# A retention layer ahead of a leaky feed-forward: state sums, visit and next scores of a pair in one run of 64x64 products

## The chip, the cores and the metric

The kernel runs on one core of one Trainium2 chip. The metric is the device time of one launch in microseconds. A core has a matrix engine (TensorE, PE in the profile, with PEld for its weight loads), two engines for elementwise work (VectorE, DVE; ScalarE, ACT), a general engine (GpSimd, POOL) and a queue that issues transfers (SyncE, SP). TensorE writes to eight PSUM banks, from which VectorE and ScalarE read.

## The reference

```python
# q, k, v: (4, 8, 768, 64); w_in: (512, 2048); w_out: (2048, 512)
gamma = 1.0 - 2.0 ** (-5.0 - np.arange(H))
for t in range(S):
    state = gamma[None, :, None, None] * state + np.einsum('bhd,bhe->bhde', k[:, :, t], v[:, :, t])
    y[:, :, t] = scale * np.einsum('bhd,bhde->bhe', q[:, :, t], state)
x = y.transpose(0, 2, 1, 3).reshape(B * S, H * D)
h = x @ w_in
g = np.maximum(0.01 * h, h)
out = g @ w_out
```

A retention layer (attention without softmax, with a decay by head) with 4 batches, 8 heads, 768 tokens and 64 dimensions a head; its output goes through two dense layers with a leaky ReLU between them.

## The kernel before

**The work.** The tokens are cut into NC = 6 chunks of C = 128. For each chunk c and batch b the retention layer needs *scores* (keys times queries within the chunk, masked to the past), *values* (masked scores times v), *reads* (the state before the chunk times the queries) and *state sums* (keys times v, added to the state). Heads have 64 dimensions, so all of these are 64x64 products: TensorE is used as four tiles of 64x64, and a product has two records in the trace. The result of a chunk, scaled by the decays gq, is the block x of 512 tokens for the dense layers. These use 128x128 weights with 128 or 256 moving columns, and save products by Strassen-like schemes of seven products (M1 to M7), hence the many sums and differences on VectorE.

**First part** (to about 223 us): chunks 0 and 1, the preparation of the weights, and the scores and visits of chunk 2, in a pool of banks of their own (`early_scores`, `early_visit`).

**Second part**: a loop over n = 0 to 15, chunk c = 2 + n // 4 and quarter u = n % 4 of the hidden units. All eight PSUM banks have fixed names, `bank[0]` to `bank[7]`. Iteration n does, in this order on TensorE: the first group of the next unit's first layer (`inner(n + 1, 0)`, banks 0 to 3, 56 records at line L1184), then, at u = 0 and 1 while a next chunk is left, a visit, then the second layer of unit n (`output`, L662, products M1, M5, M6, M2, M7, M3, M4 of 8 records each, in the rooms A, B, C, D = banks 5, 4, 7, 6), with the second group `inner(n + 1, 1)` (42 records) after the fourth of these. So visits stand at n = 0, 1, 4, 5, 8 and 9.

A *visit* makes the result of one pair of batches of the next chunk. A chunk is handled in halves of 64 tokens: the first half reads the state `old`, the second half `mid`, which is `old` plus the state sums of the first half. `value(n, crossed)` are the 8 products (16 records) of masked scores with v, for batch n of the pair, `read(n)` the reads (32 records for both halves). Products of different rows of the array may write the same place in PSUM, and are then kept in order by a marker: `rows_free` has GpSimd set a small tile to zero once the first of them have ended, and the later ones wait for that (L408). Then VectorE takes the result out of the banks and multiplies it by gq (L466).

A *run of scores* (`scores_of_pair`) follows inside output, after its third product: 64 records of scores for the pair to be visited next (L369) and 64 of its state sums (L380), in banks 0 to 3; VectorE masks the scores (L387) and adds the sums to the state (`plus`, L606). Where a chunk begins, `next_gq` moves the decays on by four small ScalarE instructions (L100).

Every engine works through its instructions in the order in which the program gives them (`manual_schedule`), and waits for others by semaphores. `outer(n + 1, 0)` is two adds on VectorE in the dense layer; `decay_v` scales v on GpSimd; `of_pair` loads the keys (kind 0) or v (kind 1) of a pair.

Of the kernel before, what the change touches and what calls it, by code (L numbers as in the profile page):

```python
# [9 lines left out]
FP32 = mybir.dt.float32  # L10
# [8 lines left out]
C = 128  # L19
# [3 lines left out]
def kernel(  # L23
# [71 lines left out]
    def next_gq():  # L95

        for j in range(2):
            for m in range(HP // 2):
                i = 2 * j + m
                nc.scalar.activation(gq[:, j, m], gq[:, j, m], AF.Identity,  # L100
                                     scale=step[:, i : i + 1])
# [251 lines left out]
    mid_of = {}  # L353
    quads = [(m, i, 2 * m + i) for m in range(HP // 2) for i in range(2)]

    def scores_of_pair(c, b, banks=None, mid=None):

        if b == 0 and c > JOINED:
            next_gq()
        banks = banks or bank  # L360
        at = [banks[j].rearrange("p (b m i t) -> p b m i t", b=2, m=HP // 2, i=2)
              for j in range(2)]
        sums = [banks[2 + h].rearrange("p (b a d) -> p b a d", b=2, a=HP) for h in range(2)]
        for n in range(2):
            x = heads[c, b + n][0]
            for m, i, a in quads:
                for h in range(2):
                    for j in range(2):
                        nc.tensor.matmul(at[j][ts(h, 64), n, m, i],  # L369
                                         lhsT=x[ts(j, 64), 1, a, ts(h, 64)],  # L370
                                         rhs=x[ts(j, 64), 0, a, ts(h, 64)],
                                         start=(n == 0 and a == 0), stop=True,
                                         skip_group_check=True)
        last = c == NC - 1
        for n in range(2):
            key, val = keys.pop((c, b + n)), vals[c, b + n]
            for a in range(HP):
                for j in range(2):
                    for h in range(1 if last else 2):
                        nc.tensor.matmul(sums[h][ts(j, 64), n, a], lhsT=key[ts(h, 64), 2 * a + j],  # L380
                                         rhs=val[ts(h, 64), 2 * a + j],
                                         start=(n == 0 and a == 0), stop=True,
                                         skip_group_check=True)
        weights = scores[c, b] = []
        for j in range(2):
            am = work.tile([128, 2, HP // 2, 2, C // 2], FP32, tag=f"am{j}", name=f"am{j}_{c}_{b}")
            nc.vector.tensor_tensor(  # L387
                out=am.rearrange("p b m i t -> p (b m i) t"),
                in0=at[j].rearrange("p b m i t -> p (b m i) t"),
                in1=mask[:, 0].unsqueeze(1).to_broadcast([128, 2 * HP, C // 2]), op=ALU.mult)  # L390
            weights.append(am)
        p = b // 2
        old = state_of[p]
        free_again[p] = [old]
        if mid is None:
            mid = halves_of_states.pop(0)
            free_again[p].append(mid)
        plus(mid, old, sums[0])
        if not last:
            state_of[p] = halves_of_states.pop(0)  # L400
            plus(state_of[p], mid, sums[1])
        mid_of[p] = old, mid
        if following(c, b) is not None and c > JOINED:
            of_pair(*following(c, b), 0)

    def rows_free(mm):

# [1 line left out]
        tc.add_manual_dep(done, mm.ins.name, IN_ORDER, reason="rows of the array")  # L409
        return done  # L410

    def joint_visit(c, b, banks=None):

        later = following(c, b) if c > JOINED else None
        banks = banks or [[bank[k] for k in at] for at in ((1, 2), (0, 7))]
        at = [[ps.rearrange("p (a t) -> p a t", t=C) for ps in of_one] for of_one in banks]
        by_half = mid_of.pop(b // 2)
        weights = scores.pop((c, b))

        def read(n, after=None):  # L420
            x = heads[c, b + n][0]
            for h in range(2):
                for m in range(HP // 2):
                    for j in range(2):
                        for i in range(2):
                            a = 2 * m + i
                            mm = nc.tensor.matmul(at[n][j][ts(i, 64), m, ts(h, 64)],  # L427
                                                  lhsT=by_half[h][ts(j, 64), n, a],
                                                  rhs=x[ts(j, 64), 0, a, ts(h, 64)],
                                                  start=(n == 0 and h == 0 and m == 0), stop=False,  # L430
                                                  skip_group_check=True)
                            if after is not None:
                                tc.add_manual_dep(mm.ins, after.name, IN_ORDER,
                                                  reason="rows of the array")
                                after = None
            return mm

        def value(n, crossed, after=None):
            val = vals[c, b + n]
            for m in range(HP // 2):  # L440
                for i in range(2):
                    for j in range(2):
                        h, a = j ^ crossed, 2 * m + i
                        mm = nc.tensor.matmul(at[n][j][ts(i, 64), m, ts(h, 64)],  # L444
                                              lhsT=val[ts(h, 64), 2 * a + j],
                                              rhs=weights[j][ts(h, 64), n, m, i],
                                              start=(n == 1 and crossed == 1 and m == 0),
                                              stop=True, skip_group_check=True)
                        if after is not None:
                            tc.add_manual_dep(mm.ins, after.name, IN_ORDER,  # L450
                                              reason="rows of the array")
                            after = None
            return mm

        done1 = rows_free(value(1, 1))
        read(0)
        done0 = rows_free(value(0, 0))
        read(1, done1)
        value(1, 0)
        value(0, 1, done0)  # L460
        for n in (1, 0):
            for j in (1, 0):
                ps = at[n][j]
                th, o = divmod((b + n) * C, N)
                blocks = xs[c][0].rearrange("p (kh th) k n -> p kh th k n", th=2)[:, :, th]
                nc.vector.tensor_tensor(out=blocks[:, j, :, ds(o, C)], in0=ps[:, 0 : HP // 2],  # L466
                                        in1=gq[:, j], op=ALU.mult)
        halves_of_states.extend(free_again.pop(b // 2))
        for n in range(2):
            heads.pop((c, b + n))  # L470
        if later is not None:
            of_pair(*later, 1)
            for n in range(2):
                decay_v(later[0], later[1] + n)

    def pair_of_banks(name):

# [2 lines left out]

    def early_scores(c, b, place):
        def do():
            banks = [pair_of_banks(f"{name}_{c}_{b}") for name in ("ap", "sp")]
            scores_of_pair(c, b, banks[0] + banks[1], place())
        return do

    def early_visit(c, b):
# [10 lines left out]
    def following(c, b):  # L498

        at = (c, b + 2) if b == 0 else (c + 1, 0)  # L500
        return at if at[0] < NC else None
# [740 lines left out]
    def products(steps, n):  # L1242

        for _ in range(n):
            next(steps, None)
# [13 lines left out]
    last = output(1, os[1], [parts[1]], False, True, room=room, order=FUSED)  # L1259
    products(last, 4)  # L1260
    halves_of_states.append(work.tile([128, 2, HP, D], FP32, tag="m5", name="half_states"))
    scores_of_pair(3, 0)
    for b in range(2):
        ahead(3, 2 + b)
    products(last, 1)
# [15 lines left out]
    for n in range(N2):  # L1281
# [9 lines left out]
        if n + 1 < N2:  # L1291
            if n > 0:
                begun = inner_steps(n + 1, 0, held=visiting)
                products(begun, 1)
            while held:
                held.pop()()
            products(begun, 7)
            outer(n + 1, 0)
        if visiting and u == 0:
            xs[c + 1] = new_x(c + 1)  # L1300
        if visiting:
            joint_visit(c + 1, 2 * u)
        steps = output(c, os[c], [gs.pop(n)], u == 0, u == NU - 1, room=room if more else last_room,
                       order=FUSED if more else LAST, held=held if more else None)
        products(steps, 3)
        if c + 1 < NC and u < 2 and following(c + 1, 2 * u):
            scores_of_pair(*following(c + 1, 2 * u))
        if visiting:
            load_unit(n + 2, 0)
        products(steps, 1)  # L1310
        if c + 1 < NC and u == 1:
            differences(*xs[c + 1])
        if c + 1 < NC and u == 2:
# [14 lines left out]
JOINED = 2  # L1328
# [87 lines left out]
```

## Time and profile before

| | |
|---|---|
| time, median of 3 | 637.88 us (637.47 to 637.89) |
| span of the profiled run | 636.0 us, TensorE clock 1.000 |
| TensorE, VectorE, ScalarE, GpSimd busy | 628.8, 464.1, 268.9, 23.3 us |
| 64x64 products of L369, L380, L427, L444 in the second part | records of 218 ns each (median), 64x64 |
| mask of scores (L387), one bank | 0.69 us |
| take of one bank (L466) | 0.415 us |
| add of 128x512 on VectorE (L606) | 0.69 us |
| ScalarE copy of a bank (L755) | 0.57 us |

Times in the page and in the answers of the trace are microseconds from the start of the span, or lengths, unless ns is written. A line of the timeline has start, length, engine, line of the kernel, operation, output and inputs with their sizes, the number of records, and in brackets how long the engine was idle before, and who ended that. Records of TensorE overlap, since a product starts before the one before it has left the array; starts are better measures than lengths.

### The profile page before, as it was taken

To read this page: it belongs to the slowest core of one execution; us is meant where nothing else is said; L and a number is where in the kernel's file an instruction comes from. 1 tells how busy PE (TensorE), PEld (TensorE's weight loads), DVE (VectorE), ACT (ScalarE), POOL (GpSimd) and SP (SyncE) were. 2 spreads that over 40 slices of the span, in tenths; PEclk is the share of its full clock that TensorE was granted. 3 is DMA by queue.
4 is the path that set the end of the run, shared out by engine and by line. 5 is a ranking of instruction groups with operands and counts; after the bars stand their busy time and mean duration, and the time that the engine had idled before them with its cause. 6 is when DMAs were issued, how large, how long until landed. Compare 5 with 4: busy or idle time off the path is not lost.

```text
span 636.0 us, 14285 instructions
## 1 busy us (share of the span) xinstructions
PE 628.8 (99%) x6086; PEld 568.8 (89%) x6086; DVE 464.1 (73%) x760; ACT 268.9 (42%) x515; POOL 23.3 (4%) x45
## 2 busy tenths in 40 slices
PE   8999999999999999999999999999999999999997
PEld 5888888888888889899999999999999999999996
DVE  5679769889979986576785666877737768636655
ACT  4876556347343124242352442423433423534421
POOL 2000000000011010101000101000010000000000
PEclk9999999999999999999999999999999999999999
DMA  8941426556863998376735392864455236444201
GB/s 331 404 131 38 128 67 220 148 174 194 283 250 110 351 333 280 103 238 193 259 88 184 120 295 79 268 195 140 137 169 185 87 123 197 154 162 158 87 1 68
DMA packets 87537, 113.42 MB, mean 178 GB/s; under 512 B 3241, under 2 KB 71721, under 8 KB 87473
## 3 DMA queue, kind: packets, MB, share of 16 engines
q1 hardware_dynamic: 87168, 111.88, 53.2%
q8 instruction: 48, 0.79, 0.5%
q10 hardware_dynamic: 304, 0.62, 0.3%
q14 instruction: 17, 0.13, 0.1%
HBM read 93.35 MB, written 19.14 MB: 177 GB/s over the span
## 4 chain that ended last, share of the span: by engine, by line
PE 95%; DVE 2%; ACT 1%; DMA 1%; issue 0%; DVEq 0%; ACTq 0%
PE bank L662 32%; PE bank L1184 27%; PE C_h L662 4%; PE B_o L662 4%; PE A_h L662 4%; PE C_o L662 4%; PE A_o L662 4%; PE B_h L662 4%; PE D_h L662 2%; PE D_o L662 2%; PE d L683 2%; PE bank L369 1%; PE bank L444 1%; PE bank L427 1%; PE bank L380 1%; DMA t<-decay_dram 1%
## 5 line engine op out<-in xcount | busy, mean ns | idle before, releaser
L606 DVE TENSOR_TENSOR made<-made,bank 128x512 f32<-128x512 f32 (+1 forms) x96 | 56.4, 618 | 55.9 <-PE bank L1184 51.5
L606 DVE TENSOR_TENSOR o<-o,bank 128x512 f32<-128x512 f32 (+2 forms) x91 | 58.5, 661 | 51.8 <-PE bank L662 31.2
L662 PE MATMUL bank<-g,w 128*128 128x256 f32 x384 | 89.9, 382 | 0.0
L662 PEld LDWEIGHTS bank<-g,w 128*128 128x128 f32 x384 | 70.7, 190 | 9.2
L1184 PEld LDWEIGHTS bank<-x,wb 128*128 128x128 f32 x672 | 77.6, 192 | 0.8
L1184 PE MATMUL bank<-x,wb 128*128 128x128 f32 x672 | 77.6, 275 | 0.0
L1184 PE MATMUL bank<-x,wa 128*128 128x128 f32 x512 | 67.7, 275 | 0.0
L662 PE MATMUL bank<-gd,w 128*128 128x256 f32 x288 | 66.1, 379 | 0.0
L1184 PEld LDWEIGHTS bank<-x,wa 128*128 128x128 f32 x512 | 63.5, 192 | 1.1 <-ACT made L1194 0.2
L662 PEld LDWEIGHTS bank<-gd,w 128*128 128x128 f32 x288 | 54.7, 190 | 7.4
L1184 PE MATMUL bank<-t,wa 128*128 128x128 f32 x384 | 53.3, 275 | 0.0
L1226 ACT ACTIVATE g<-g 128x512 f32<-128x512 f32 x64 | 39.3, 631 | 30.8 <-DVE g L606 30.8
L1184 PEld LDWEIGHTS bank<-t,wa 128*128 128x128 f32 x384 | 48.0, 192 | 0.0
L1188 ACT COPY bank<-bank 128x512 f32<-128x512 f32 (+1 forms) x32 | 16.7, 520 | 67.8 <-PE bank L1184 67.5
L606 DVE TENSOR_TENSOR g<-made 128x512 f32<-128x512 f32 x64 | 42.7, 688 | 1.2
L755 ACT COPY bank<-bank 128x512 f32<-128x512 f32 x17 | 9.7, 570 | 71.2 <-PE bank L662 71.1
L609 DVE TENSOR_TENSOR gd<-g,gd 128x512 f32<-128x512 f32 x48 | 33.2, 692 | 5.4 <-ACT g L1226 0.5
L776 ACT COPY bank<-bank 128x512 f32<-128x512 f32 x16 | 9.1, 570 | 46.4 <-PE bank L662 46.4
L662 PE MATMUL bank<-g,last 128*128 128x256 f32 x120 | 28.3, 380 | 0.0
L662 PE MATMUL bank<-gd,last 128*128 128x256 f32 (+1 forms) x124 | 27.5, 373 | 0.0
L662 PE MATMUL A_h<-x,w 128*128 128x256 f32 x112 | 26.6, 380 | 0.0
L662 PEld LDWEIGHTS bank<-gd,last 128*128 128x128 f32 x124 | 22.8, 190 | 3.2 <-DVE gd L609 0.3
(223 smaller groups left out, 1030.1 us busy)
## 6 DMA issues: line engine op xcount, KB each, us to landing
wa<-kept SPq DMA_DIRECT2D x16, 1344.0 KB, 7.2
raw<-in_weights_dram SPq DMA_DIRECT2D x31, 512.0 KB, 4.4
wb<-kept SPq DMA_DIRECT2D x16, 896.0 KB, 5.7
wa<-kept SPq DMA_DIRECT2D x16, 448.0 KB, 4.4
wb<-kept SPq DMA_DIRECT2D x16, 448.0 KB, 6.3
out_dram<-o SPq DMA_DIRECT2D x23, 256.0 KB, 3.1
kept<-w SPq DMA_DIRECT2D x12, 448.0 KB, 6.0
qk<-in_qk_dram SPq DMA_DIRECT2D x10, 512.0 KB, 8.0
```

The costliest lines, as they stand in the source:

```text
L369: nc.tensor.matmul(at[j][ts(h, 64), n, m, i], lhsT=x[ts(j, 64), 1, a, ts(h, 64)], rhs=x[ts(j, 64), 0, a, ts(h, 64)], start=(n == 0 and a = ...
L380: nc.tensor.matmul(sums[h][ts(j, 64), n, a], lhsT=key[ts(h, 64), 2 * a + j], rhs=val[ts(h, 64), 2 * a + j], start=(n == 0 and a == 0), sto ...
L427: mm = nc.tensor.matmul(at[n][j][ts(i, 64), m, ts(h, 64)], lhsT=by_half[h][ts(j, 64), n, a], rhs=x[ts(j, 64), 0, a, ts(h, 64)], start=(n = ...
L606: nc.vector.tensor_tensor(out=out, in0=a, in1=b, op=ALU.add)
L609: nc.vector.tensor_tensor(out=out, in0=a, in1=b, op=ALU.subtract)
L662: nc.tensor.matmul(to, lhsT=block(w, sa)[:, k, ts(i, 128)], rhs=rhs[:, k, a:z], start=(first and (i == 0 or split) and n == 0 and k == 0), ...
L683: nc.tensor.matmul(banks[r][:, i, :], lhsT=block(2 * u, r + 2 * kh)[:, k, ts(i, 128)], rhs=x[:, 2 * kh + th, k, :], start=(step == 0 and i ...
L755: nc.scalar.copy(out=bank_of("B"), in_=ps)
L776: nc.scalar.copy(out=bank_of("D"), in_=ps)
L1184: nc.tensor.matmul(ps[q][:, i], lhsT=w[:, j, i], rhs=part_of(moving[i], s), start=(i == 0 and m in ("M1", "M5", "M4")), stop=True, skip_gr ...
L1188: nc.scalar.copy(out=ps[3], in_=ps[0])
L1226: nc.scalar.activation(g[:, i], g[:, i], AF.Prelu, alpha=0.01)
```

## The change

`scores_of_pair` is cut into its parts: `scores_of` (the products of the scores), `sums_of_states`, `masked_pair` and `new_states`. The state sums of a pair now come at the head of its own visit, and the scores of the next pair inside that visit, so that all 64x64 products of an iteration of the second part are one run (`long_visit`). It is for having TensorE change between 128x128 and 64x64 products less often. Ahead of the loop only the scores of (3, 0) remain.

The order of the run: state sums (64 records, banks 5 and 4), value(1,1), value(0,1), value(1,0), value(0,0) (16 each), the reads of the first half for both batches (16 each), the next pair's scores (64, banks 6 and 3), the reads of the second half (16 each). Before, it was value(1,1), read(0), value(0,0), read(1), value(1,0), value(0,1), and the scores and sums apart. The visit's own banks stay 1 and 2 for batch 0, 0 and 7 for batch 1.

VectorE's order changes with it: the state adds, then a mask, the take of bank 7, the other mask, the takes of banks 0, 1 and 2, and only then the two adds of `outer(n + 1, 0)`, which stood ahead of the takes. `next_gq` comes ahead of output's first ScalarE copy instead of behind it, and keys and v of the next pair are loaded together after the visit.

```diff
+    def long_visit(c, b, behind):
+
+        later = following(c, b)
+        sums = sums_of_states(c, b, (bank[5], bank[4]))
+        new_states(c, b, sums)
+        read, value, taken = of_visit(c, b, [[bank[k] for k in at] for at in ((1, 2), (0, 7))])
+        done = [rows_free(value(n, 1)) for n in (1, 0)]
+        for n in (1, 0):
+            value(n, 0, done[1 - n])
+        for n in (1, 0):
+            read(n, (0,))
+        if later is not None:
+            at = scores_of(*later, (bank[6], bank[3]))
+        for n in (1, 0):
+            read(n, (1,))
+        places = [(1, 1), (1, 0), (0, 0), (0, 1)]
+        if later is not None:
+            masked_pair(*later, 0, at)
+            taken(*places.pop(0))
+            masked_pair(*later, 1, at)
+        for place in places:
+            taken(*place)
+        visited(c, b)
+        behind()
+        if later is None:
+            return
+        if later[1] == 0:
+            next_gq()
+        for kind in (1, 0):
+            of_pair(*later, kind)
+        for n in range(2):
+            decay_v(later[0], later[1] + n)
...
-    scores_of_pair(3, 0)
+    at = scores_of(3, 0, bank[0:2])
+    next_gq()
+    for j in range(2):
+        masked_pair(3, 0, j, at)
...
             products(begun, 7)
-            outer(n + 1, 0)
         if visiting and u == 0:
             xs[c + 1] = new_x(c + 1)
         if visiting:
-            joint_visit(c + 1, 2 * u)
+            long_visit(c + 1, 2 * u, lambda: outer(n + 1, 0))
+        elif more:
+            outer(n + 1, 0)
...
-        products(steps, 3)
-        if c + 1 < NC and u < 2 and following(c + 1, 2 * u):
-            scores_of_pair(*following(c + 1, 2 * u))
         if visiting:
             load_unit(n + 2, 0)
-        products(steps, 1)
+        products(steps, 4)
```

## The prediction

> **What bounds the kernel now.** I read the page's busy times and chain first: whose time is it?
>
> ```profile
> PE 628.8 (99%) x6086; PEld 568.8 (89%) x6086; DVE 464.1 (73%) x760; ACT 268.9 (42%) x515; POOL 23.3 (4%) x45
> ...
> PE 95%; DVE 2%; ACT 1%; DMA 1%; issue 0%; DVEq 0%; ACTq 0%
> ```
>
> TensorE is the bound, and the 5% that isn't TensorE lies mostly before the second part. So a change there is worth exactly what it takes from or adds to TensorE's line of work. Second, the chain in order of time (start, length, line, records) over iterations n=1 and n=2 of the second part:
>
> ```profile
> 277.39 6.25 PE bank L1184 x56
> 285.66 5.38 PE bank L662 x24
> 291.04 1.09 PE bank L369 x64
> 293.06 1.92 PE bank L662 x8
> 294.99 4.69 PE bank L1184 x42
> 299.68 5.18 PE bank L662 x24
> 304.86 6.25 PE bank L1184 x56
> 311.11 6.91 PE bank L662 x32
> 318.02 4.69 PE bank L1184 x42
> 322.71 5.18 PE bank L662 x24
> 327.89 6.25 PE bank L1184 x56
> ```
>
> An iteration without a visit lasts 327.89 - 304.86 = 23.03 us, and no gap is in it. One with a visit (the hole between 283.64 and 285.66) and a run of scores (291.04 to 293.06) lasts 304.86 - 277.39 = 27.47 us, so the two runs of 64x64 products cost 4.44 us. Third, the timeline around that visit, TensorE and GpSimd:
>
> ```profile
> 283.57 0.46 PE L444 MATMUL bank<-am,v 64*64 64x64 f32 x16
> 284.18 0.10 POOL L408 MEMSET between<- 128x1 f32 x1 [20.24 <-PE bank L444]
> 284.32 0.41 PE L444 MATMUL bank<-am,v 64*64 64x64 f32 x16
> 284.55 0.41 PE L427 MATMUL bank<-o,more_states 64*64 64x64 f32 x16
> 285.02 0.65 PE L444 MATMUL bank<-am,v 64*64 64x64 f32 x32
> 285.59 1.99 PE L662 MATMUL bank<-g,w 128*128 128x256 f32 x8
> ```
>
> From 284.32 to 285.02 are 48 records: 14.6 ns each (a 64x64 product has two records). The two runs together have 256 records, 3.74 us, so 4.44 - 3.74 = 0.70 us, **0.35 us a run, is the price of going into 64x64 products and out again**. The last visit, which has no scores after it, agrees: its iteration lasts 25.25 us in the chain, 2.22 over the clean one, which is 128 x 14.6 ns + 0.35.
>
> Fourth, where a visit stood still. Visits n=0 and n=5 are longer than the 2.02 us of n=1:
>
> ```profile
> 256.33 0.69 PE L427 MATMUL bank<-qk,states 64*64 64x64 f32 x32 [0.18 <-DVE made L606]
> ```
>
> ```profile
> 386.02 0.84 PE L444 MATMUL bank<-am,v 64*64 64x64 f32 x32
> ```
>
> ```profile
> 386.24 0.10 POOL L408 MEMSET between<- 128x1 f32 x1 [0.96 <-PE bank L444]
> ```
>
> Visit n=0 waits for VectorE to leave bank 1 (255.69 to 258.12, 2.43 us: 0.41 lost). At n=5 a marker memset comes late, and TensorE waits 0.19 us for it. This shows the path TensorE, GpSimd, TensorE: the memset ends at 386.34, and the second half of those 32 records, due at 386.25, starts 0.19 later, at 386.44. So TensorE goes on 0.10 us after the memset's end.
>
> [...]
>
> **Part 1, one run in place of two.** The second part had 12 runs (scores and state sums of (3,0) ahead of the loop, six visits, five runs of scores and sums). It will have 7: scores of (3,0), then six long visits. The number of products is the same. Five runs fewer: 5 x 0.35 = -1.75 us. At n=0 the bank that VectorE was late with is first touched after 64 records of state sums and 16 of values (1.17 us) instead of 0.28, and the wait was 0.4: -0.41. The run ahead of the loop took 230.66 to 232.82, 2.16 us against 2.03 for 290.97 to 293.00; its late half moves: -0.13. **Gain 2.29 us**.
>
> **Part 2, the wait for the memsets.** Before, between a group of 16 values and the products that wait for its memset lay 48 records, 0.70 us. Now the order is value(1,1), value(0,1), value(1,0): only 16 records lie between. A group ends 0.41 us after its start in a run (its row's length), the memset starts 0.15 later (284.03 to 284.18), takes 0.10, and TensorE goes on 0.10 after: 0.76. It would have been there after 32 records, 0.47. **Stall 0.29, say 0.30 us, in each of six visits: +1.80.** What is queued behind: all the rest of the run, and behind that output's first product, so the path itself. The second memset is due 0.23 after the first and GpSimd is free by then, so I count nothing for it. Bounds: with no time for TensorE to see the semaphore, 0.19 a visit (1.1 us); with a full second turn as well, 0.60 (3.6 us). Late memsets are new on the path too: of the 16 in the trace one came 0.35 late and one lasted 0.41 for 0.10; 12 x 2/16 x 0.3 = 0.45, less the 0.19 that n=5 paid before: +0.26.
>
> **Part 3, the scalings of gq.** They stood behind output's first copy on ScalarE and cost nothing:
>
> ```profile
> 287.62 0.57 ACT L755 COPY bank<-bank 128x512 f32<-128x512 f32 x1 [5.15 <-PE bank L662]
> 288.11 1.28 ACT L100 ACTIVATE dec<-dec 128x128 f32<-128x128 f32 x4
> ```
>
> Now they stand ahead of that copy, at the visits whose next pair begins a chunk (n=1 and n=5), and they wait for the takes on VectorE that read gq. Clock from the run's start: the run is 0.05 + 3.74 + 0.30 + 0.10 = 4.19, M1 then starts, M5 at +1.83 and M6 at +1.73, 7.75. Scores begin at 0.05 + 160 x 14.6 ns + 0.30 = 2.69; a mask starts 1.21 later (290.97 to 292.18 in the trace), 3.90. VectorE then has two masks (0.60 apart) and four takes (0.33 apart, 0.415 long): last two takes start at 5.76 and 6.09. ScalarE's first scalings start at 6.20, four times 0.30 later, 7.40, the copy of 0.57 starts, and M6 may start at 7.40 + 0.57 + 0.05 = 8.02 instead of 7.75: **0.27 us, twice: +0.54**. Bounds: 0 and 0.5 each.
>
> **Costs nothing.** The state adds on VectorE end near 2.9 us after the run's start (sums adds until 1.4, then two, the second 0.78 after the first's start); the reads that need them come at 3.6, the 64 records of scores hide them. Bank 3 is free at 1.4, the scores come at 2.7. Bank 7 is taken by 4.9, M5 needs it at 6.0. Banks 5 and 4 are free by 2.9, M1 and its copy come at 4.2 and later. outer's two adds move behind the takes (to 7.9): what uses them is over ten microseconds off. Keys and values of the next pair are loaded together after the visit, 3.7 us to land and 2.04 of decays, against over 20 us until they are read; scores of (3,2) move 7 us forward, their input was issued at 235.33. The weights' load is issued some 6 us earlier.
>
> **Sum.** -2.29 + 1.80 + 0.26 + 0.54 = +0.31: 637.88 becomes **638.2 us**, no difference to speak of: five mode switches saved, and paid back at the memsets.
>
> **Rivals.** A, faster: the wait for the memsets is mostly hidden [...]: -2.29 + 0.54 = -1.75, 636.1 us. For it: five switches are certainly gone, and the path's latency comes from one stalled visit. Against it: GpSimd's 0.15 + 0.10 is the same at nearly every visit. B, slower: both memsets cost a full turn, 0.6 a visit, and the copy on ScalarE comes 0.5 late: -2.29 + 3.6 + 0.26 + 1.0 = +2.57, 640.5 us; half of that excess gives 639.4. For it: two of sixteen memsets were irregular, and two will follow closely. Against it: before, GpSimd was ready again after 0.1.
>
> **Chances.** Forecast 0.57, A 0.17, B 0.26. The bound of 0.2% is 1.28 us (636.6 and 639.16), so faster 0.17, same 0.57, slower 0.26. The range goes from A's centre, 636.1, to a little short of B's, 640.0; half of A and somewhat under half of B are left out.
>
> **What would show it.** Right: iterations with a visit and scores last 27.47 - 0.35 + 0.30 = 27.4 us at n=4 and 8 and 27.7 at n=1 and 5; in each long visit the third group of 16 values starts about 0.76 after the first; at n=1 and 5 M6 follows the copy. Wrong: no gap there (then A), gaps before both groups (then B), or a wait for VectorE at the second reads or at M5, which I count at nothing.

## The result, and the profile after

The changed kernel takes **643.3 us** (median of 5 runs, 642.98 to 646.0), the kernel before 637.88 (637.47 to 637.91) beside it: ratio 1.0097, 95% interval 1.0076 to 1.0118. The forecast was 638.2 with a range up to 640.0. The change costs about 5.4 us, and 5.1 of them stood in no step of the forecast.

The page of the kernel after, for the totals: busy times by engine, the transfers of instructions (queue, how many, MB, share of the span), and the shares of the chain of waits.

```profile
PE 632.8 (98%) x6086; PEld 571.9 (89%) x6086; DVE 462.6 (72%) x760; ACT 269.0 (42%) x515; POOL 23.1 (4%) x45
...
q8 instruction: 48, 0.79, 0.5%
...
PE 93%; DMA 2%; ACT 1%; DVE 1%; issue 1%; POOL 0%; POOLq 0%
```

The number of products is the same, 6086, and TensorE is still the bound. "issue", time in which an engine waits for nothing that the profile shows, was 0% of the chain and is now 1%. A share on the page doesn't say where it lies; the chain in order of time does. Iteration n=1 (start, length, engine and line, records):

```profile
276.42 6.25 PE bank L1238 x56
282.67 1.09 PE bank L379 x64
283.76 0.28 PE bank L452 x15
...
284.16 0.11 POOL between L410
...
284.31 0.70 PE bank L452 x32
285.01 0.47 PE bank L434 x32
285.47 0.93 PE bank L364 x64
286.41 0.34 PE bank L434 x22
286.75 2.96 issue
289.71 0.58 PE bank L434 x7
290.30 9.75 PE bank L716 x32
...
309.92 6.25 PE bank L1238 x56
...
365.03 0.10 PE bank L364 x5
365.13 0.42 issue
365.55 1.09 PE bank L364 x58
...
367.16 7.10 PE bank L716 x32
...
467.33 0.85 PE bank L364 x57
468.18 0.55 issue
```

The iteration lasts 309.92 - 276.42 = 33.50 us, where it lasted 27.47 before. The memset on GpSimd (L410) stands between two groups of values, as forecast. But then TensorE stops for 2.96 us in the middle of the second reads, with no engine named. Two smaller stops of the same kind lie in the scores of n=4 (0.42) and n=8 (0.55). And the first 32 records of output (L716) take 9.75 us at n=1, while the same records take 7.10 at n=4. The reason is the clock. Windows of the kernel after (stretch, length, busy time of PE, PEld, DVE, ACT and POOL with their instructions, granted clock, share of the DMA engines, GB/s):

```profile
280.00:288.80 8.80, 6.67 (x270) 6.28 (x270) 6.04 (x11) 1.23 (x3) 1.24 (x4) 1.00 0.40 104
288.80:295.60 6.80, 5.88 (x23) 4.69 (x23) 2.04 (x4) 1.85 (x5) 1.00 (x1) 0.50 0.87 294
295.60:310.00 14.40, 14.40 (x90) 13.27 (x89) 9.09 (x15) 4.18 (x8) 0.00 (x0) 1.00 0.29 87
```

From 288.80, some 2 us into the stop of 2.96, TensorE is granted 0.50 of its clock for 6.80 us, and 1.00 in the stretches before and after: 9.75 - 7.10 = 2.65 us lost. Not every execution has it: three of the five kept the clock at 1.000, with spans of 641.0 to 641.3 us against 644.2 here. The run of the median, 643.3, is one of these three, so it doesn't contain the half clock, and its excess over the forecast is about what the other entries of the table below add up to; the 646.0 of the profiled execution contains both.

By iteration (start of the first group to the start of the next, from the two traces; the forecast's column follows from its steps, at n=0 28.18 - 0.35 - 0.41 + 0.30). "Restart" is what a stop costs beyond its idle time: at n=1 the starts of two records lie 3.18 us apart, and the idle time between them is 2.96.

```
n        before   forecast   after    after - forecast, and what it is
0        28.18    27.7       28.04    +0.3   0.3 waiting for weights (wa)
1        27.47    27.7       33.50    +5.8   stop 2.96, half clock 2.65, restart 0.2
4        27.47    27.4       28.16    +0.7   stop 0.42, restart 0.2
5        27.66    27.7       28.11    +0.4   second memset late 0.3, scalings of gq 0.1
8        27.47    27.4       28.21    +0.8   stop 0.55, restart 0.2
9        25.25    26.48      26.47     0.0
others   23.03    23.03      23.03     0.0
```

Iteration n=9, whose long visit has no scores, is on the forecast: 25.25 + 0.93 for the state sums that moved in + 0.30 for the memset. The runs don't all have 256 records, as the forecast has them: of the last chunk only one half of the state sums is needed, 32 records instead of 64, all on the same rows of the array. They take the same 0.93 us (29 ns a record), so the forecast's times stand, but the run has 224 records at n=8 and 160 at n=9. So the arithmetic of times, mode changes and memsets holds, and most of the excess lies in stops inside runs of 224 and 256 records.

### The profile page after: what moved, and what is told of

The parts are those of the page before. It is cut to its first block, busy times and chain, and to the rows that moved or that the text cites. A ratio compares the mean times of both kernels' runs of the same rounds, so it can differ in the third digit from the quotient of the medians.

```text
span 644.2 us, 14278 instructions
## 1 busy us (share of the span) xinstructions
PE 632.8 (98%) x6086; PEld 571.9 (89%) x6086; DVE 462.6 (72%) x760; ACT 269.0 (42%) x515; POOL 23.1 (4%) x45
## 4 chain that ended last, share of the span: by engine, by line
PE 93%; DMA 2%; ACT 1%; DVE 1%; issue 1%; POOL 0%; POOLq 0%
PE bank L716 31%; PE bank L1238 26%; PE C_h L716 4%; PE B_o L716 4%; PE A_h L716 4%; PE C_o L716 4%; PE A_o L716 4%; PE B_h L716 4%; PE D_o L716 2%; PE D_h L716 2%; PE d L737 2%; DMA wa<-kept 1%; PE bank L379 1%; PE bank L364 1%; PE bank L452 1%
## 5 line engine op out<-in xcount | busy, mean ns | idle before, releaser
L716 PE MATMUL bank<-g,w 128*128 128x256 f32 x384 | 91.2, 386 | 0.0
L716 PEld LDWEIGHTS bank<-g,w 128*128 128x128 f32 x384 | 72.2, 193 | 9.5
L716 PE MATMUL bank<-gd,w 128*128 128x256 f32 x288 | 67.3, 383 | 0.1
L716 PEld LDWEIGHTS bank<-gd,w 128*128 128x128 f32 x288 | 55.5, 193 | 8.2 <-ACT bank L809 0.5
L716 PE MATMUL bank<-g,last 128*128 128x256 f32 x120 | 28.3, 380 | 0.0
L716 PE MATMUL bank<-gd,last 128*128 128x256 f32 (+1 forms) x124 | 27.5, 373 | 0.0
L716 PE MATMUL A_h<-x,w 128*128 128x256 f32 x112 | 26.6, 380 | 0.0
L716 PEld LDWEIGHTS bank<-gd,last 128*128 128x128 f32 x124 | 22.8, 190 | 3.2 <-DVE gd L663 0.3
```

Source lines behind the costliest of these rows:

```text
L716: nc.tensor.matmul(to, lhsT=block(w, sa)[:, k, ts(i, 128)], rhs=rhs[:, k, a:z], start=(first and (i == 0 or split) and n == 0 and k == 0), ...
```

## The experiments

Two theories stood against each other first. **F**: the loads of keys, v and weights, which the change issues during the run, hold TensorE up. **L**: the length of the run does it, whatever is being loaded. The timeline of the kernel after gives F its case:

```profile
283.85 0.33 SPq L136 DMA_DIRECT2D v<-in_kv_dram  x1
...
285.12 0.33 SPq L136 DMA_DIRECT2D k<-in_kv_dram  x1
...
285.49 0.53 SPq L1115 DMA_DIRECT2D wa<-kept  x1
...
286.23 0.52 PE L434 MATMUL bank<-o,states 64*64 64x64 f32 x22
...
289.71 0.58 PE L434 MATMUL bank<-o,states 64*64 64x64 f32 x10 [2.96 <-issue]
```

**e1_loads_later**: all these loads wait for output's third product, where the kernel before issued its last ones.

```diff
-        nc.sync.dma_start(out=place, in_=kv[c, b + kind])
+        behind_products(nc.sync.dma_start(out=place, in_=kv[c, b + kind]))
...
-            nc.sync.dma_start(out=wa[:, :, 0:1], in_=kept[u][:, :, 0:1])
+            behind_products(nc.sync.dma_start(out=wa[:, :, 0:1], in_=kept[u][:, :, 0:1]))
...
-        products(steps, 4)
+        products(steps, 3)
+        if visiting:
+            behind[0] = latest[0]
+        while after_run:
+            after_run.pop()()
...
+        products(steps, 1)
```

> The long run kept as it is; the loads of the next pair's keys and v and of the first group's weights wait for output's third product, some 5 us after the run's end. Theory F (TensorE's own instructions come by transfers of 16 KB, and these stand behind the loads that are issued inside the run): TensorE's unexplained gaps in the long runs vanish, and the time falls from 643.1 by about 4.5 to 638.0 to 639.2 us. Theory L (256 records in a row use up instructions faster than they can be fetched, loads or not): gaps and time stay, 642 to 643.5. Theory M (the wait for the memsets and the scalings, mis-sized): the same as L.

Measured: 641.96 us (641.16 to 642.94), 1.0064 [1.0049, 1.0079]. Its chain in order of time:

```profile
286.19 0.34 PE bank L441 x22
286.53 0.99 issue
287.51 0.39 PE bank L441 x7
...
359.99 0.10 PE bank L371 x5
360.09 0.86 issue
360.95 1.09 PE bank L371 x58
```

The stop at n=1 falls from 2.96 to 0.99, the clock stays, but a stop is left at n=1, and at n=4 and n=8 they are 0.86 and 0.79. They stand at the same records as in the kernel after: 22 records into the second reads, 5 into the scores. At n=4 and n=8 the stop even grew. So the loads lengthen the stop at n=1; they don't make it.

**e8_before_wa_early**: the kernel before, with the weights' load moved ahead of output, to where the change has it.

```diff
             joint_visit(c + 1, 2 * u)
+            load_unit(n + 2, 0)
...
-        if visiting:
-            load_unit(n + 2, 0)
```

> The kernel before with one line moved: the first group's weights (1.8 MB) are loaded right behind the visit instead of behind the run of scores, so that this load is under way during the run of scores (128 records, 5 us after the visit). Theory F in its simple form (any run meets it): gaps in the runs of scores, 639 to 641 us. Theory F with a stock of instructions [...] and theory L: no gaps, 637.9.

Measured: 637.73 us (12 runs), 1.0 [0.9989, 1.0011], and every iteration as long as before but n=0 (28.30 for 28.18, where TensorE waits 0.15 for weights). An early load with runs of 128 records costs next to nothing.

**x_before_double**: the kernel before, where each run of scores and sums is issued twice in a row, 256 records (192 at n=5 and n=8, for the last chunk). The second pass writes the same results again.

```diff
+        for turn_of in range(2 if c > JOINED else 1):
+            for n in range(2):
+                x = heads[c, b + n][0]
...
```

> The kernel before, where only the run of scores and state sums is lengthened: its 128 records are issued twice in a row, the second time with the same operands into the same places (the result is the same, the work is not needed). No load is moved; keys and weights are still loaded only behind this run. Six runs, 128 records x 14.6 ns x 6 = 11.2 us more in any case, 649.1. Theory L (two instruction blocks have to come within a run of 256 records, and one takes longer than 128 records last): gaps of 0.4 to 1.0 us with no releaser in most of the six runs, 651.5 to 654. Theory F (it is the loads alone): no such gaps, 648.8 to 649.5.

Measured: 660.1 us (659.69 to 661.57), 1.0354 [1.0336, 1.0373]; the added products alone are 6 x 128 x 14.6 ns = 11.2 us at most. Its chain at n=1 and n=4:

```profile
297.13 1.09 PE bank L371 x64
298.22 0.93 PE bank L381 x64
299.16 0.45 PE bank L371 x28
299.61 1.08 issue
300.70 0.74 PE bank L371 x34
...
376.89 0.21 PE bank L381 x10
377.11 1.18 issue
378.29 1.04 PE bank L381 x54
```

A kernel without the change, with no memset in its run and no load issued during it, stops as the changed one does. All six doubled runs stop (0.59 to 1.38, and 2.42 at n=8, where v and the weights had been issued some 5 us ahead, and where half clock follows: output's next 8 records take 3.59 us for 1.92). The total is above L's 651.5 to 654. Apart from the added products the work ahead of the loop and the five iterations with a doubled run are 10.7 us longer than in the kernel before, of which the six stops are 7.4; the rest is their restarts and the half clock. L had the cause and too small a price.

**x_before_twice_apart**: nearly the same additional work (a second and third set of scores, overwritten later), as a run of its own with one product of output (1.73 us) between it and the real run.

```diff
-        products(steps, 3)
+        products(steps, 2)
+        if c + 1 < NC and u < 2 and following(c + 1, 2 * u):
+            products_of_pair(*following(c + 1, 2 * u))
+        products(steps, 1)
```

> The counterpart to the doubled run: the kernel before with as many products more (the 64 records of scores, twice, results not used), but as a run of their own of 128 records, one of output's products (8 records of 216 ns, 1.7 us) ahead of the run of scores. Six runs more, each 128 x 14.6 ns + 0.35 us: 13.3 us, 651.2. Theory L (it is the length in one piece that outruns the instruction blocks): no gap without a releaser over 0.2 us, 650.9 to 652. If it is the sheer number of products in an iteration: gaps as in the doubled run, 658 or more.

Measured: 652.56 us (651.94 to 656.75), 1.0228 [1.0212, 1.0244]. The timeline of TensorE at n=1:

```profile
294.00 2.10 PE L367 MATMUL bank<-qk 64*64 64x64 f32 x128
296.02 1.99 PE L679 MATMUL bank<-gd,w 128*128 128x256 f32 x8
297.95 1.16 PE L386 MATMUL bank<-qk 64*64 64x64 f32 x64
298.93 1.11 PE L397 MATMUL bank<-v,k 64*64 64x64 f32 x64
```

No stop at n=0, 1, 4 and 5: iterations of 30.40, 29.69, 29.69 and 29.88, which at n=1 is 27.47 + 128 x 14.6 ns + 0.35 for one more mode change. So 256 records cost their price if 1.7 us of larger products stand between them. Two stops are left that L hadn't expected: 0.17 us ahead of the loop, and 1.99 us at n=8, in the product between the two runs, where v and 1.8 MB of weights had been issued some 3 us ahead of the block that ends there.

**What runs out.** The pages of the kernel before and of the kernel after have 48 instruction transfers, 0.79 MB in all, which is 16 KB each, for 12,172 records on TensorE (products and weight loads, 6086 of each): 254 records a transfer. The pages of the two kernels with about 1,400 and 1,500 records more have 53 and 54. And the three stops of the kernel after begin behind TensorE's instructions 6081, 7361 and 9665, counted from the start of the trace: 1280 and 2304 apart, 5 and 9 times 256. So I take 256 instructions as the content of a transfer of 16 KB, and call them a block. When do the blocks come? In the second part of every run a block's transfer starts 3.2 us or more after the second block before it has begun (4.57 at the least in the kernel before, 4.00 in the kernel after), so no trace shows one that comes earlier than that. Each record of a product comes with one of a weight load, so 128 records of 64x64 products are one block, and at 14.6 ns a record a run eats a block in 1.87 us.

Whether that is the cause can be counted. In each trace I numbered TensorE's instructions (products, weight loads and what else it executes) from the start. In ten traces (the kernel after, e1 to e7 and both x kernels) there are 38 stops of the second part, over 0.33 us from one start to the next, for which the trace names no engine and which are not single records at half clock (0.42 to 0.43 us apart in the kernel after); **every one of the 38 comes after an instruction whose number is 193 modulo 256**, and TensorE goes on 1.23 to 1.59 us after the 16 KB transfer has ended. The kernel before, e8_before_wa_early and e9_before_bank6 have none. In x_before_double the stops stand at other records of the run than in the kernel after, and still at this number. Four of them, and the same place in the kernel before, with the start of the block's 256 instructions, of the transfer that the next block needs, its end, and the time at which TensorE reaches the next block:

```
kernel, n            block begun   transfer starts   ends     next block   stop
before, 1            284.34        285.04            285.98   291.38       none
after, 1             284.65        287.30            288.28   289.71       2.96
after, 4             362.69        363.22            364.24   365.55       0.42
e1_loads_later, 1    284.43        285.16            286.25   287.51       0.99
e1_loads_later, 4    357.65        358.23            359.58   360.95       0.86
```

So with no load issued ahead of it a block takes, in these traces, 0.5 to 0.7 us until its transfer starts (1.1 at n=1 and n=4 of e5_all below), 0.9 to 1.4 for the transfer, 1.2 to 1.6 until TensorE goes on: some 3 us in all (in e1_loads_later 3.08 at n=1 and 3.30 at n=4, from the start of one block to the next), against 1.87 that a run gives it. A run of 128 records holds one block end and has the slower 128x128 products (8 records of output in 1.73 us) before or after it; inside the loop of the kernel before the shortest block lasted 4.90 us. (Ahead of the loop one lasted 2.81 without a stop; there the transfer for the next had started 0.23 us before the block began.) A run of 256 holds two ends. At n=1 of the kernel after the transfer started 2.65 us after its block had begun instead of 0.7: v was issued 0.8 us ahead of that beginning, keys and weights 0.5 us and more after it.

Do loads delay the transfer of a block? **e6_kv_later** holds back only keys and v, so that 1.8 MB of weights are issued just ahead of the run.

```diff
+        after_run.append(lambda: loads_of(later))
...
         if visiting:
             load_unit(n + 2, 0)
-        products(steps, 4)
+        products(steps, 3)
+        if visiting:
+            behind[0] = latest[0]
+        while after_run:
+            after_run.pop()()
```

> The long run as it is, keys and v held back until output's third product, but the first group's weights (1.8 MB), no longer queued behind them on the issuing engine, start at once when the first group is done, that is at the head of the long run, ahead of the request for the block that n=1, 4 and 8 run out of. Theory F for the loads' part (a block of instructions stands behind what was issued before it was asked for): gaps at n=1, 4 and 8 of 2 us or more each, over those of 0.8 to 1.0 with all loads held back; 645 to 650 us. If only keys and v matter (their place, not their being first): gaps as with both held back, 641.5 to 642.5.

Measured: 654.96 us (651.82 to 656.08), 1.0253 [1.0219, 1.0287]. Its timeline at n=1:

```profile
285.63 0.52 SPq L1130 DMA_DIRECT2D wa<-kept  x1
286.31 0.56 SPq L1131 DMA_DIRECT2D wa<-kept  x1
...
289.83 0.52 PE L441 MATMUL bank<-o,states 64*64 64x64 f32 x22
...
294.70 0.43 PE L441 MATMUL bank<-o,states 64*64 64x64 f32 x10 [4.35 <-issue]
```

The block begun at 288.26 had its successor's transfer start at 292.19, 3.93 us later, and the stop at the same record is 4.35. The other iterations with a next pair, n=0, 4, 5 and 8, last 29.6 to 30.05, each with a stop at a block's end, two of them (n=0 and n=5) where the kernel after had none; the total is above the 645 to 650 expected. With these 1.8 MB ahead of it the block came later than with v's 0.5 MB ahead of it in e7_wa_later below (2.50 us). The kernel before shows such a delay without the cost: in e8_before_wa_early a transfer at n=1 starts 2.37 us after its block has begun instead of 0.59, and the block, 5.56 us long, hides it.

**e7_wa_later** is the other half: only the weights wait.

```diff
-            nc.sync.dma_start(out=wa[:, :, 0:1], in_=kept[u][:, :, 0:1])
+            behind_products(nc.sync.dma_start(out=wa[:, :, 0:1], in_=kept[u][:, :, 0:1]))
...
+        products(steps, 3)
+        if visiting:
+            behind[0] = latest[0]
```

> Of the two loads that the change issues inside the long run, only the weights (1.8 MB) wait for output's third product; keys and v (1 MB) still start inside the run. Theory F for the part that loads have: if the weights are what the instruction block stands behind, n=1's gap is about 1.0 us, as with both loads moved, and the time 641.5 to 642.3; if keys and v are enough, the gap stays over 2 us, 643 to 644.

Measured: 645.68 us (643.76 to 648.59), 1.0125 [1.0092, 1.0158]; n=1 has a stop of 2.67 and half clock (output's 32 records in 8.68 us for 7.10). Keys and v, 0.5 MB each, issued 0.8 us ahead of the block's beginning and 0.5 after it, delay the transfer by themselves, to 2.50 us after it, where it was 0.73 in e1_loads_later. The kernel isn't faster than the kernel after.

**e2_scores_apart**: the scores go back behind output's third product, with the loads as in the change. Runs are 192 and 64 records (160 and 64 at n=8).

```diff
-        if later is not None:
-            at = scores_of(*later, (bank[6], bank[3]))
...
-        products(steps, 4)
+        products(steps, 3)
+        if visiting and following(c + 1, 2 * u):
+            at = scores_of(*following(c + 1, 2 * u), (bank[6], bank[3]))
+            for j in range(2):
+                masked_pair(*following(c + 1, 2 * u), j, at)
+        products(steps, 1)
```

> The changed kernel, with the next pair's scores (and their masks) taken out of the long run and put back behind output's third product: runs of 192 and 64 records; the loads stay where the change put them. Five mode changes more, +1.75. Theory L: the gap stands at a block's end, so at n=1, where it was 246 records into the run, it goes; at n=4 and n=8 it was 165 and 185 records in, which is still inside 192, so there it stays, 0.4 to 1.2 us each. Time 641.5 to 643. Theory F: loads are issued at the same time as before, so gaps at the same three visits, longest at n=1: 644.5 to 645.

Measured: 641.45 us (640.97 to 642.83), 1.0058 [1.0042, 1.0074]. n=1 is 27.78 and n=8 27.76, without a stop, which is the memset's 0.31 over the kernel before. n=4 keeps 0.40, since there two block ends still fall into the 192 records. At n=8 a stop had been expected too, 185 records into a run of 192; the run has 160. (n=0 has 29.39, most of it 0.84 of waiting for weights, a mode change and a stop of 0.17.) Where block ends fall in a run decides, not the length alone.

Three runs tested what the forecast had priced.

**e3_values_first**: value(1,1) and value(0,1) go ahead of the state sums, so that 64 records lie between a group and the products that wait for its memset.

```diff
-        sums = sums_of_states(c, b, (bank[5], bank[4]))
-        new_states(c, b, sums)
         read, value, taken = of_visit(c, b, [[bank[k] for k in at] for at in ((1, 2), (0, 7))])
         done = [rows_free(value(n, 1)) for n in (1, 0)]
+        sums = sums_of_states(c, b, (bank[5], bank[4]))
+        new_states(c, b, sums)
```

> Only the order of products is changed: value(1,1), value(0,1), then the 64 records of state sums, then the rest, so that the memsets have 0.93 us more. All theories: the gap of 0.30 us before the third group of values goes, 6 x 0.30 = -1.8 us, 641.3. Theory M would have more of the 5 us here: 639.5 or less. Theory F and L: the unexplained gaps stay, one of them may even grow by what is saved, so 641.3 to 642.3.

Measured: 643.81 us (642.69 to 647.2), 1.0101 [1.0071, 1.013]. The stop at the memset is gone, and nothing is won, against 641.3 to 642.3 expected. Its waits of TensorE (line, whom it waited for, us in total, times, longest):

```profile
PE bank L715 <- issue: 2.3, 2, 2.1
PE bank L364 <- issue: 1.9, 2, 1.2
PE bank L433 <- issue: 1.4, 2, 1.2
```

A run that gets on faster only reaches the end of its block earlier: n=4 stops 1.15 us where the kernel after stops 0.42, and n=5, which had none, 2.08 (in output, L715). At n=0 the wait for VectorE comes back (0.4), since the values touch bank 1 early again, and 0.8 are waited for weights. n=9, with 160 records, keeps a gain: 26.26 instead of 26.47.

**e4_gq_later**: `next_gq` comes behind output's first copy again.

```diff
         if later[1] == 0:
-            next_gq()
+            behind_copy.append(next_gq)
...
-        products(steps, 4)
+        products(steps, 1)
+        while behind_copy:
+            behind_copy.pop()()
+        products(steps, 3)
```

> Only the scalings of gq move back behind output's first copy on ScalarE. Predicted step: -0.54 us (2 x 0.27). In the trace of the changed kernel M6 waited 0.5 us at n=5 alone, so -0.5 to -1.0: 642.1 to 642.6. Theory F: at n=1, where VectorE's takes are late because TensorE stood still, a little more. None of the theories expects over 1.2 us.

The timeline of ScalarE at n=5, in the kernel after and then in this one:

```profile
396.84 1.28 ACT L100 ACTIVATE dec<-dec 128x128 f32<-128x128 f32 x4 [7.62 <-DVE x L467]
398.02 0.57 ACT L809 COPY bank<-bank 128x512 f32<-128x512 f32 x1
```

```profile
395.63 0.57 ACT L811 COPY bank<-bank 128x512 f32<-128x512 f32 x1 [7.67 <-PE bank L718]
396.11 1.28 ACT L100 ACTIVATE dec<-dec 128x128 f32<-128x128 f32 x4
```

The copy comes first, and n=5 falls from 28.11 to 27.77, by 0.34. The total, 643.81 us (643.05 to 644.58), 1.0088 [1.0071, 1.0105], isn't lower, against 642.1 to 642.6 expected: at n=1 and n=4 it stops for 2.62 and 0.86.

**e5_all** has all three edits: loads later, values first, gq later.

```diff
-        sums = sums_of_states(c, b, (bank[5], bank[4]))
-        new_states(c, b, sums)
...
+        sums = sums_of_states(c, b, (bank[5], bank[4]))
+        new_states(c, b, sums)
...
-            next_gq()
+            behind_copy.append(next_gq)
+        after_run.append(lambda: loads_of(later))
```

> The long run with all three repairs: loads behind output's third product, value(1,1) and value(0,1) ahead of the state sums, scalings of gq behind output's first copy. From the 642.0 of the loads alone. Theory L: at n=1, 4 and 8 what the memsets no longer cost is given back at the block's end; at n=0, 5 and 9 0.3 each is saved, 0.4 more for a late memset, and about 1.0 at the scalings: 639.6 to 640.4, slower than the kernel before. If the memset's waits are worth their full price at all six visits: 638.6 to 639.0.

Measured: 641.72 us (641.12 to 642.64), 1.006 [1.0044, 1.0076], the same as e1_loads_later alone and above the 639.6 to 640.4 expected. Stops of 1.39 (n=1), 1.36 (n=4) and 0.65 (n=8) are left. At n=1 the 1.39 is e1_loads_later's 0.99 and about the 0.31 of the memset: what is saved in the run is waited for at the block's end. n=5, n=8 and n=9 gain (27.47 for 28.09 in e1_loads_later, 28.00 for 28.46, 26.27 for 26.47), n=4 loses 0.2, and n=0 loses 1.1: 0.6 to the weights, 0.4 to VectorE at bank 1 and 0.4 to a new stop, less the memset's 0.3.

**e9_before_bank6** tested the wait for VectorE at n=0, in the kernel before: the visit's batch 0 uses bank 6 instead of bank 1. (As I read the program, in half of that bank M4 then replaces what M7's copy left instead of adding to it, so this kernel leaves out a part of the layer's sum; products and their order are the same.)

```diff
-        banks = banks or [[bank[k] for k in at] for at in ((1, 2), (0, 7))]
+        banks = banks or [[bank[k] for k in at] for at in ((6, 2), (0, 7))]
```

> The kernel before, where a visit's batch 0 uses banks 6 and 2 instead of 1 and 2, so that visit n=0 needn't wait for VectorE to leave bank 1. Runs stay 128 records long. n=0's iteration 0.4 us shorter (28.18 to 27.8), nothing else changed: 637.4 us.

Measured: n=0 falls from 28.18 to 27.79, by 0.39; the total, 637.65 us (21 runs), 0.9994 [0.9988, 1.0001], can't be told from no change.

No arrangement tried beats the kernel before. With no stop an iteration with a long run would last 23.03 + 256 x 14.6 ns + 0.35 = 27.12 us against 27.47; the shortest one measured was 27.47 (n=5 of e5_all).

## Why the prediction was wrong

**The step that failed** is the length of the run: "the run is 0.05 + 3.74 + 0.30 + 0.10 = 4.19", with 3.74 = 256 x 14.6 ns, and with it Part 1, where one run in place of two was a pure gain of a mode change. 14.6 ns was measured in a run of 128, and I carried it to 256 as if the stream of instructions could never end. In its place the runs showed stops at the ends of instruction blocks: 2.96, 0.42 and 0.55 us at n=1, 4 and 8, and some 0.2 in each restart, 4.5 us in all where the step had nothing. The kernel before can't show such a stop, because it has none; but its page, too, has the 48 transfers of instructions, and dividing 12,172 instructions by 48 shows that a run of 256 products' records uses two of them up in 3.74 us.

**A line of "Costs nothing"** failed with it: "The weights' load is issued some 6 us earlier", and keys and v together after the visit. I asked only when their readers need them. They stand ahead of the transfer of instructions: some 2 us of the stop at n=1 (2.96 against 0.99 in e1_loads_later), and through the long stop the half clock, 2.65 us, in some executions. In the kernel before the weights' load, early, costs next to nothing (e8_before_wa_early), since there the blocks have time to spare.

**Part 1, the terms beside it.** The mode change of 0.35 us a run held: x_before_twice_apart pays 2.22 for 1.87 of records. VectorE's wait at n=0 held (0.39 in e9_before_bank6 for 0.41). But the work ahead of the loop is shorter, so TensorE comes to inner(1, 0) some 0.8 us earlier and waits 0.3 us there for its weights (0.6 to 0.8 in e5_all, e2_scores_apart, e3_values_first and e7_wa_later): part of the gain ahead of the loop is waited away.

**Part 2, the memset, was right**: the third group of values starts 284.31 - 283.58 = 0.73 us after the first (0.76 in the forecast), a stop of about 0.3 in each visit. Visit n=0 lasts 4.26 us for 4.19. The second memset costs nothing, except at n=5. The allowance for late memsets, 0.26, was close to the 0.3 us that one cost, but it took for chance what comes back at one place: the second memset of n=5 (idle before it 0.96 us in the kernel before, 0.49 after, 0.47 in e1_loads_later). Why it is late stays open.

**Part 3, the scalings of gq, was right**: 0.34 us at n=5 (e4_gq_later) for 0.27. At n=1 of the kernel after the stop hid it: its own scalings ended at 291.99, and the copy, which waited for TensorE, started at 294.04.

**The rivals.** A (memset hidden) fell; its premise, a stop of nearly nothing, is met only by e3_values_first and e5_all, where the block ends take most of the gain back. B had the right side and the wrong cause: it doubled the memset. The second memset and VectorE at the second reads, which I named as the places where it would go wrong, stayed quiet; the stop did come at the second reads, but with no engine behind it. All rivals varied waits between engines, and none a limit of TensorE's own supply.

## What to carry to other kernels

Small products cost instructions as well as array time: before joining runs of them, divide a block of instructions by the rate at which they are used, and see whether the next block can come in that time (here some 3 us were needed, and 1.87 given). Stops with no engine named ("issue") whose instruction numbers differ by multiples of a block (256 here), and transfers of instructions on the page (48), were the sign; larger products between two runs were then worth more than the mode change that they cost (652.56 us in x_before_twice_apart, 660.1 in x_before_double). And a load's place isn't free because its reader is far off: ask what else has to be transferred at that moment (here a block of instructions, whose transfer started 3.93 us into the block before it with 1.8 MB of weights issued ahead, and 0.73 with no load ahead).

## What the runs showed of the hardware

- In these traces TensorE's instructions come in blocks of 16 KB (48 transfers, 0.79 MB), 256 at a time, and it stops where they are used up before the next have come (all 38 stops stand at one number modulo 256, and TensorE goes on 1.23 to 1.59 us after the transfer). In the loop before the change, with 4.90 us and more a block, it never stopped for one; in runs with 1.87 us a block there were stops of 0.65 to 1.39 us with no load in the way (n=1, 4 and 8 of e1_loads_later and e5_all).
- The transfer of such a block came later where loads had been issued before it: it started 0.5 to 1.1 us after its block had begun without them (e1_loads_later and e5_all, at the stops of n=1, 4 and 8), 2.50 with v ahead of it and keys just after (e7_wa_later), 3.93 with 1.8 MB of weights ahead (e6_kv_later). Some transfers started before the block ahead of theirs had begun (at n=0 and n=5 of the kernel after, by 0.16 and 0.30 us), and then there was no stop, or a small one (0.22 at n=0 of e5_all, where it came about as early); what decides that stays open.
- After some stops of 2 to 3 us TensorE ran at half clock: after 2.96 in the kernel after (0.50 granted for 6.80 us), after 2.42 in x_before_double (8 records of output in 3.59 us for 1.92) and after 1.99 in x_before_twice_apart (64 records of scores in 1.82 us for 1.09). After 2.08 in e3_values_first (23 records of output in 5.12 us) and 2.38 in e6_kv_later (32 in 7.11) it didn't, nor after the longest of the shorter stops, 1.86 in e6_kv_later (32 in 7.10). What decides it, these runs don't show.
